# One hand-written order for six batches: every relu, square, sum and copy at a place of its own, and a PSUM bank named for each matmul group

## The chip, the cores and the metric

The kernel runs on one core of one Trainium2 chip. The metric is device time in microseconds (us), the median of the runs shown. Engines are called PE (TensorE, matmuls), DVE (VectorE), ACT (ScalarE), POOL (GpSimd) and SP (SyncE, here a queue that issues DMAs).

## The reference

There are 8 batches, 12 heads, 448 positions and a head size of 64; then a feed-forward layer over 3584 tokens, from 768 to 2048 and back to 768.

```python
scores = scale * np.matmul(q, k.transpose(0, 1, 3, 2))
attn = np.maximum(scores, 0.0) ** 2 / S
attn_out = np.matmul(attn, v)              # (B, H, S, D)
x = attn_out.transpose(0, 2, 1, 3).reshape(B * S, H * D)
h = x @ w_in
g = np.maximum(h, 0.0) + alpha * np.minimum(h, 0.0)
out = g @ w_out
```

## The kernel before

All work is written out in one order by hand. Each engine runs its own instructions strictly in the order in which they stand, and waits by semaphore for what other engines must give. So the order of the words in the plan strings is the order in every queue.

**Attention.** Four heads of one batch are a quad; there are 24 quads, three to a batch. `turn_dma` copies a quad's q and k into the tile `perm` (one buffer) and lets a DMA on SP's queue turn it into the tile `T`; `land` is a tiny POOL copy that waits for that DMA, and behind it POOL issues the loads of quads to come. A quad has seven chunks. A chunk (`c` in the plans, lines 204 to 221) is four matmuls of 64x64 weights that run side by side, here called one group of four, into two neighbouring PSUM banks (a pair); then a relu out of both banks, on ACT or DVE as the letter says; and, later, `s` squares it (line 229 or 231). When all seven chunks of a quad are squared, `v` (line 241) multiplies them with v: seven groups of four into one pair, and two copies (lines 253 and 255) take the pair to the tile `xT`, one bank on ACT and one on DVE.

**First layer.** When a batch's three quads are in `xT`, sixteen units `f` follow: six matmuls (line 275) into one bank, then ACT makes `neg` (line 281; two buffers) and DVE writes `gT` (line 282). `gT` holds two batches.

**Second layer.** The 28 tiles of 128 tokens are mostly taken in pairs. A pair is multiplied by a scheme with seven products of half size in place of eight: `p1` to `p7` on PE (line 335, 8 matmuls of 384 columns each), sums of parts of `gT` on DVE (`pa` to `pd`, line 331), and after each product a copy on ACT (lines 351 and 356) or an addition on DVE (line 340). Products 2, 3, 4 and 5 give blocks of the output, which `store` sends with two DMAs each. Four tiles go the plain way (`g`, line 300).

**PSUM.** There are 8 banks. `take_pair` gives the pair that was taken longest ago, `one` a single bank by the same rule. In the last six batches `one` first tries the other half of the pair that was used last (the flag `paired`), so that pairs stay whole. A plan word does a whole step at once: `cA` issues the matmuls and the relu, `f` the matmuls, `neg` and `gT`, `p6` the product and its addition.

**The order.** The first two batches and the start have plans of their own. Then batch by batch the strings `FIRST_PAIR`, `EACH`, `EACH`, `ONE_PAIR`, `EACH` and `LAST` run, each from `B`: its units `f` first, then its products, with the chunks of later quads in between, mostly three at a time (`cAAA`), and the three `v` of the next batch. This is `EACH`:

```python
EACH = """B f s0D f s0A f n f f f f s2A f s1D cAAA s1D f f s0D f s0A f p1 nD f f r1 f f s1A pc p2 pa r2 ra pb cA vDA s1D s0D cAA p6 s0D pd p7 n cA rc s1A cAA s0D s0A p5 p4 rb p3 cAAD v cAD s1D s1A s3A cA s3A r6 s2A r7 rd r5 s0A cAD r4 s0D r3 cAD v cD cA"""
LAST = """B f s0A f f f f s3A s2A s2A f f s2A f f f f f f pc f f s0A f p1 r1 pa pb p2 p6 p7 pd ra p5 rb rc p4 p3 r6 z r7 rd r5 r2 r3 r4e"""
```

Here `r` is the second pair of the batch, `n` is `turn_dma`, `land` and the next loads, `z` puts every second store from then on into ACT's queue, and `r4e` makes the last product in two parts, 256 and 128 columns wide. A `c` behind the last chunk, an `s` with nothing to square and an `n` behind the last quad do nothing.

Of the kernel before, what the change touches and what calls it, by code (L numbers as in the profile page):

```python
# [20 lines left out]
def kernel(  # L21
# [72 lines left out]

    def one():
        order = sorted(range(8), key=lambda i: (taken[i], i))
        free = [i for i in order if taken[i] < 10**9]
        if not paired:
            return order[0]
        mate = max(free, key=lambda i: taken[i]) ^ 1  # L100
        return mate if mate in order[:4] and taken[mate] < 10**9 else order[0]
# [86 lines left out]
    def turn_dma(n, eng="A"):  # L188
        if n in (5, 7, 8):
            w = w_mix[2 + n % 2].rearrange("p k c -> p (k c)")[:, :4 * NJ * D]  # L190
            p = w.rearrange("p (a j s d) -> p a j s d", a=2, j=NJ, s=2)
        else:
            p = perm_pool.tile([128, 2, NJ, 2, D], BF16, tag="perm", name="perm")
        for i, name in enumerate("qk"):
            (nc.vector.tensor_copy if eng == "D" else nc.scalar.copy)(p[:, i], raw.pop((n, name)).rearrange("p s j d -> p j s d"))  # L195
# [1 line left out]
        nc.sync.dma_start_transpose(out=t.rearrange("p a j c -> p (a j) c"),
                                    in_=p.rearrange("p a j s d -> p (a j s d)"))
# [35 lines left out]
    def attnv(n, eng="AD"):  # L234
        ps = take_pair()
        vv = vraw.pop(n)
        for j in range(NJ):
# [10 lines left out]
        if eng == "A":
            nc.scalar.activation(xT[b][:, g], ps[:, :, :S], ACTF.Copy, scale=out_scale)
            return  # L250
        for r in range(2):
            if eng[r] == "A":
                nc.scalar.activation(xT[b][:, g, r], ps[:, r, :S], ACTF.Copy, scale=out_scale)  # L253
            else:
                nc.vector.tensor_scalar(xT[b][:, g, r], ps[:, r, :S], out_scale, None, ALU.mult)  # L255
# [15 lines left out]
    gT = singles.tile([128, KF, 2 * S], BF16, name="gT")  # L271

    def f1_mm(ps, b, ff, ks):
        for km in ks:
            nc.tensor.matmul(ps, w_in_sb[:, km // 2, km % 2, bass.ts(ff, 128)],  # L275
                             xT[b][:, km // 2, km % 2, :],
                             start=(km == 0), stop=(km == KM - 1))

    def f1_out(ps, b, ff):
        neg = neg_pool.tile([128, S], F32, tag="neg", name="neg")  # L280
        nc.scalar.activation(neg, ps, ACTF.Relu, scale=-1.0)  # L281
# [11 lines left out]
    def f2(sb, c, h, parts=None):  # L293

        first_col, width = COLS[h][0], COLS[h][1] - COLS[h][0]
        o = o_pool.tile([128, d_model - CUT], F32, tag="o", name="osb")
        for lo, hi in parts or ((0, width),):
            ps = take_bank()[:, :hi - lo]
            for ff in range(KF):
                nc.tensor.matmul(ps, gT[:, ff, bass.ts(c, 128)], w_out_sb[:, ff, first_col + lo:first_col + hi],  # L300
                                 start=(ff == 0), stop=(ff == KF - 1))
            nc.scalar.copy(o[:, lo:hi], ps)
            store(sb, c, first_col + lo, first_col + hi, o[:, lo:hi])
# [11 lines left out]
    class Pair:  # L315

        def __init__(self, a, b):
            self.a, self.b = a, b
# [14 lines left out]
        def mm(self, ps, left, right, start):  # L333
            for i in range(KH):
                nc.tensor.matmul(ps, left[:, i], right[:, i], start=(start and i == 0), stop=(i == KH - 1),  # L335
                                 skip_group_check=not start)

        def plus(self, ps, u, keep=None):
            t = keep if keep is not None else o_pool.tile([128, d_model - CUT], F32, tag="o", name="osb")[:, :u.shape[-1]]
            nc.vector.tensor_tensor(t, ps, u, ALU.add)  # L340
            return t

        def kept(self, tag="u"):
            return u_pool.tile([128, NH], F32, tag=tag, name=tag)

        def p1(self):
            self.xb = hold()
            self.x = psum[:, self.xb, :NH]
            self.mm(self.x, self.a11, w_out_sb[:, :KH, :NH], True)
            self.m1 = self.kept("m")  # L350
            nc.scalar.copy(self.m1, self.x)

        def p2(self):
            self.mm(self.x, self.a12, w_out_sb[:, KH:, :NH], False)
            t = o_pool.tile([128, d_model - CUT], F32, tag="o", name="osb")[:, :NH]
            nc.scalar.copy(t, self.x)  # L356
            take(self.xb, 1)
            store(*self.a, 0, NH, t)

        def p6(self):  # L360
            y = take_bank()[:, :NH]
            self.mm(y, self.s[2], w_mix[1], True)
            self.u2 = self.plus(y, self.m1, self.kept())

        def p7(self):
            y = take_bank()[:, :NH]
            self.mm(y, self.s[3], w_mix[2], True)
            self.u3 = self.plus(y, self.u2, self.kept())

        def p5(self):  # L370
            self.zb = hold()
            self.z = psum[:, self.zb, :NH]
            self.mm(self.z, self.s[1], w_mix[0], True)
            store(*self.b, NH, d_model, self.plus(self.z, self.u3))

        def p4(self, parts=((0, NH),)):
            for lo, hi in parts:
                y = take_bank()[:, :hi - lo]
                self.mm(y, self.a22, w_mix[3][:, :, lo:hi], True)
                t = self.plus(y, self.u3[:, lo:hi])  # L380
                store(*self.b, lo, hi, t)

        def p4x(self, lo=0, hi=256):
            if lo == 0:
                self.o4 = o_pool.tile([128, d_model - CUT], F32, tag="o", name="osb")[:, :NH]
            y = take_bank()[:, :hi - lo]
            self.mm(y, self.a22, w_mix[3][:, :, lo:hi], True)
            self.plus(y, self.u3[:, lo:hi], self.o4[:, lo:hi])
            if hi == NH:
                store(*self.b, 0, NH, self.o4)  # L390

        def p4y(self):
            self.p4x(256, NH)

        def p4e(self):
            self.p4(((0, 256), (256, NH)))

        def p3(self):
            self.mm(self.z, self.s[4], w_out_sb[:, KH:, NH:], False)
            store(*self.a, NH, d_model, self.plus(self.z, self.u2))  # L400
            take(self.zb, 1)
# [150 lines left out]
```

## Time and profile before

| what | us |
|---|---|
| median of 3 runs | 373.29 (373.25 to 375.82) |
| span of the profiled execution | 371.3 |
| median of the runs less that span | 2.0 |
| start of batch 2's first `f` in the profile | 109.2 |

The profile is of one execution and its span runs from the first to the last instruction on the core. A matmul's time in it is longer than its distance to the next one, since matmuls are pipelined; what counts for PE is the distance from start to start. In a timeline a row begins with the start and the length of a run of like instructions; x48 says how many; brackets hold how long the engine was idle before and what released it.

### The profile page before, as it was taken

What the parts mean: (1) busy time and instruction counts of PE and PEld (TensorE: products, weight loads), DVE (VectorE), ACT (ScalarE), POOL (GpSimd) and SP (SyncE); (2) the same over time, 40 slices, a digit from 0 to 9 for tenths busy, and PEclk for the clock granted to TensorE, in tenths of its full rate; (3) what the DMA queues carried; (4) which work ended last, traced back from release to release, by engine and by line L of the source; (5) the groups of instructions that cost most, each with busy time, mean ns of one, the idle gap of its engine ahead of it and who ended that gap; (6) DMA issues with size and microseconds to landing.
All of it is one profiled execution on the core that took longest, in us unless ns stands there. A gap on an engine that the chain in (4) does not pass through costs nothing.

```text
span 371.3 us, 7894 instructions
## 1 busy us (share of the span) xinstructions
PE 363.6 (98%) x3105; PEld 197.5 (53%) x3105; DVE 278.0 (75%) x445; ACT 274.7 (74%) x406; POOL 71.7 (19%) x120
## 2 busy tenths in 40 slices
PE   8799999999999999999999999999999999999995
PEld 6454564444554565545555455554555455555563
DVE  3989988885968989566887768888749667856653
ACT  5998676877997678885997859967699866964400
POOL 8566150304211222022020220202200000000000
PEclk9999999999999999999999999999999999999999
DMA  9999989999999868455882659727646201220024
GB/s 143 188 203 202 199 135 191 153 160 167 180 171 150 123 96 163 92 89 90 160 144 64 99 80 168 144 56 121 111 89 134 49 2 43 65 65 0 0 64 108
DMA packets 73557, 43.29 MB, mean 117 GB/s; under 512 B 40368, under 2 KB 73008, under 8 KB 73520
## 3 DMA queue, kind: packets, MB, share of 16 engines
q0 software_dynamic: 27136, 22.58, 42.0%
q1 hardware_dynamic: 45712, 19.61, 25.9%
q10 hardware_dynamic: 672, 0.59, 0.5%
q8 instruction: 24, 0.39, 0.4%
q14 instruction: 13, 0.11, 0.1%
HBM read 45.62 MB, written 11.01 MB: 153 GB/s over the span
## 4 chain that ended last, share of the span: by engine, by line
PE 94%; DVE 2%; ACT 2%; issue 1%; ACTq 0%
PE psum L275 38%; PE psum L335 30%; PE psum L241 9%; PE psum L209 9%; PE psum L300 6%; PE psum L183 1%; PE psum L165 1%; DVE gT L282 1%; ACT rl L218 1%; ACT xT L253 1%; ACT neg L281 1%; DVE w_mix L195 1%; DVE T L186 0%; DVE at L231 0%; DVE osb L340 0%
## 5 line engine op out<-in xcount | busy, mean ns | idle before, releaser
L275 PE MATMUL psum<-xT,w_in_sb 128*128 128x448 bf16 x768 | 150.4, 353 | 0.2 <-DVE gT L282 0.2
L282 DVE SCALAR_TENSOR_TENSOR gT<-neg,beta_sb,psum 128x448 bf16<-128x448 f32 x128 | 85.3, 679 | 43.4 <-ACT neg L281 42.1
L218 ACT ACTIVATE rl<-psum 128x896 bf16<-128x896 f32 x128 | 111.2, 925 | 6.7 <-PE psum L209 4.7
L275 PEld LDWEIGHTS <-w_in_sb 128*128 128x128 bf16 x768 | 73.4, 98 | 73.0 <-issue 6.8
L281 ACT ACTIVATE neg<-psum 128x448 f32<-128x448 f32 x128 | 68.5, 547 | 41.0 <-PE psum L275 32.7
L231 DVE TENSOR_TENSOR at<-rl 128x896 bf16<-128x896 bf16 x105 | 62.2, 620 | 0.5 <-ACT rl L218 0.2
L229 ACT ACTIVATE at<-rl 128x896 bf16<-128x896 bf16 x63 | 58.6, 952 | 0.3
L335 PEld LDWEIGHTS <-S 128*128 128x128 bf16 x384 | 36.7, 98 | 28.4 <-issue 5.3
L335 PE MATMUL psum<-w_mix,S 128*128 128x384 bf16 x288 | 49.8, 326 | 0.2
L220 DVE TENSOR_SCALAR rl<-psum 128x896 bf16<-128x896 f32 x40 | 43.2, 1086 | 8.7 <-PE psum L209 8.1
L209 PE MATMUL psum<-T 64*64 64x448 bf16 x672 | 45.9, 357 | 2.0 <-DVE T L186 1.0
L418 POOL COPY landed<-T 1x1 bf16<-1x1 bf16 x18 | 3.3, 181 | 206.1 <-DMA T<-perm 182.9
L335 PEld LDWEIGHTS <-gT 128*128 128x128 bf16 x296 | 28.3, 98 | 20.2 <-issue 1.8
L241 PE MATMUL psum<-at,vraw 64*64 64x448 bf16 x672 | 36.6, 350 | 0.0
L335 PE MATMUL psum<-w_out_sb,gT 128*128 128x384 bf16 x192 | 34.0, 326 | 0.0
L340 DVE TENSOR_TENSOR osb<-psum,u 128x384 f32<-128x384 f32 (+2 forms) x37 | 20.2, 547 | 12.6 <-PE psum L335 8.2
L209 PEld LDWEIGHTS <-T 64*64 64x64 bf16 x672 | 17.4, 105 | 22.7 <-issue 14.8
L241 PEld LDWEIGHTS <-vraw 64*64 64x64 bf16 x672 | 21.2, 106 | 11.9 <-issue 2.9
L300 PE MATMUL psum<-w_out_sb,gT 128*128 128x256 bf16 (+1 forms) x128 | 22.0, 326 | 0.1
L255 DVE TENSOR_SCALAR xT<-psum 128x448 bf16<-128x448 f32 x24 | 14.9, 622 | 8.9 <-PE psum L241 8.3
L253 ACT ACTIVATE xT<-psum 128x448 bf16<-128x448 f32 x24 | 13.3, 556 | 9.1 <-PE psum L241 8.7
L356 ACT COPY osb<-psum 128x384 f32<-128x384 f32 x12 | 5.8, 480 | 17.4 <-PE psum L335 17.4
(45 smaller groups left out, 242.0 us busy)
## 6 DMA issues: line engine op xcount, KB each, us to landing
out_dram<-osb SPq DMA_DIRECT2D x91, 96.0 KB, 2.2
vraw<-in_v_dram POOLq DMA_DIRECT2D x24, 224.0 KB, 6.5
qraw<-in_q_dram POOLq DMA_DIRECT2D x23, 224.0 KB, 4.1
kraw<-in_k_dram POOLq DMA_DIRECT2D x23, 224.0 KB, 5.3
w_in_sb<-in_moe_w_in_dram POOLq DMA_DIRECT2D x16, 192.0 KB, 8.0
w_out_sb<-in_moe_w_out_dram POOLq DMA_DIRECT2D x4, 512.0 KB, 9.5
w_out_sb<-in_moe_w_out_dram POOLq DMA_DIRECT2D x4, 256.0 KB, 8.8
out_dram<-osb SPq DMA_DIRECT2D x8, 128.0 KB, 3.2
```

The lines of the kernel that those rows point to most:

```text
L209: nc.tensor.matmul(ps[64 * c:64 * c + 64, r, :S], t[64 * r:64 * r + 64, 1, j, 64 * c:64 * c + 64], t[64 * r:64 * r + 64, 0, :, 64 * c:64 * ...
L218: nc.scalar.activation(rl, ps[:, :, :S], ACTF.Relu)
L220: nc.vector.tensor_scalar(rl, ps[:, :, :S], 0.0, None, ALU.max)
L229: nc.scalar.activation(a, rl, ACTF.Square)
L231: nc.vector.tensor_tensor(a, rl, rl, ALU.mult)
L241: nc.tensor.matmul(ps[64 * s:64 * s + 64, r, :S], vv[64 * r:64 * r + 64, s, j, :], a[64 * r:64 * r + 64, s], start=(j == 0), stop=(j == NJ ...
L275: nc.tensor.matmul(ps, w_in_sb[:, km // 2, km % 2, bass.ts(ff, 128)], xT[b][:, km // 2, km % 2, :], start=(km == 0), stop=(km == KM - 1))
L281: nc.scalar.activation(neg, ps, ACTF.Relu, scale=-1.0)
L282: nc.vector.scalar_tensor_tensor(gT[:, ff, (b % 2) * S:(b % 2) * S + S], neg, beta_sb[:, ff:ff + 1], ps, ALU.mult, ALU.add)
L300: nc.tensor.matmul(ps, gT[:, ff, bass.ts(c, 128)], w_out_sb[:, ff, first_col + lo:first_col + hi], start=(ff == 0), stop=(ff == KF - 1))
L335: nc.tensor.matmul(ps, left[:, i], right[:, i], start=(start and i == 0), stop=(i == KH - 1), skip_group_check=not start)
L340: nc.vector.tensor_tensor(t, ps, u, ALU.add)
```

## The change

The plans of the start and of batches 0 and 1 stay as they are, word for word in effect. The six strings from `FIRST_PAIR` to `LAST` are replaced by one list, `P[4]`, for which a class `Line` has one short function per operation. Each operation has a word of its own, and a digit names the bank:

```diff
+        def do_f(self, w):          # "f4": six matmuls into bank 4
+            i = int(w)
+            self.bank[i] = self.b, self.ff, psum[:, i, :S]
+            f1_mm(psum[:, i, :S], self.b, self.ff, range(KM))
...
+        def do_N(self, w):          # "N4": neg of bank 4, on ACT
...
+        def do_G(self, w):          # "G4": gT from bank 4, on DVE
...
+        def do_c(self, w):          # "c6": chunk into banks 6 and 7
+        def do_r(self, w):          # "r6A": its relu, on ACT
+        def do_s(self, w):          # "sD": the oldest open square, on DVE
+        def do_v(self, w):          # "v2": into banks 2 and 3
+        def do_x(self, w):          # "x20A": bank 2's half to xT, on ACT
+        def do_k(self, w):          # "kqD", "kkD": copy of q or of k into perm
+        def do_t(self, w):          # transpose DMA, land, the next loads
...
+        def product(self, w):       # "+b63": pair b, product 6, bank 3
+        def output(self, w):        # "-b6": its copy or addition, and its store
+        def mix(self, w):           # "*bc": one sum of parts of gT
+        def do_g(self, w):          # "g2505": plain tile, bank 5;  "h5": its copy
```

The pairs of tiles are the same twelve, called a to l. The list:

```
*bc f0 sA *ba N0 *bb f1 f2 +b63 kqA f4 kkD G0 N1 sA N2 G1 sA c6 N4 G2 -b6 c0 c2 r6A sD G4 f5 r0A f4 N5 N4 sD f6 sD G5 f7 t c0 G4 sA N6 r2D N7 G6 kqD
c4 r0A r4A sD v2 kkA c0 x20A f6 sD x21A f4 N6 sD f5 G7 f7 r0D G6 N4 t c2 N5 G4 G5 sD N7 r2A G7 c0 c4 r0A sD f6 f7 f2 f3 sD N6 N7 G6 kqD r4A N2 sD G7
kkA c0 c4 r0A v6 N3 G2 r4D x60A G3 *bd c0 x61D r0A sA sD t c4 +b72 +b53 -b7 c0 c6 sA sD r4A r0A sA +c12 r6D -b5 sA +b44 +b33 c6 r6A *ca sD kqD -b4 c0
-c1A v4 kkD x40A r0D c6 t -b3 r6D c0 x41A +c22 sD -c2A sA sD f3 r0D c4 N3 f2 r4A c6 sD G3 c0 r6D c4 r0A kqD kkD sA *cc f3 f0 f1 N3 N2 G3 t N1 G2 N0
r4A sD G1 f6 N6 f7 f1 G0 f0 sD N7 G6 G7 c2 c4 N1 G1 v6 r2A c2 r4D kqD N0 c4 r2A x60A f1 r4A f2 N1 sD f3 sD kkD sD G0 x61A G1 N2 c4 c6 sD f0 sD f1 r4A
N3 G2 r6A f2 G3 f3 N0 *cb c4 N1 G0 G1 sD sA N2 r4A N3 c6 G2 v0 r6D x00A G3 c4 t c6 x01A r4A +c72 +c63 *da r6A kqD sD +c50 sD sA -c6 -c7 *cd sA -c5 c4
kkD r4A c6 *db *ea sD t c2 r6A +d11 +c44 c6 -c4 r2A +c30 sD sA c2 r6A -d1A sD r2D c4 r4A -c3 v6 x60A *dc c4 c2 x61D +d60 sD +d21 r4D -d6 c6 r2A c2 *dd
kqD c4 sA +d70 r6A kkD +d56 -d2A +d47 -d7 sA sA r2D sA -d5 r4A sD +d36 c0 sA r0D -d3 c2 v4 sD r2A x40A c0 -d4 c2 sA f6 r0A f7 r2D x41A N6 *eb sD c2 sD
c0 N7 t r2A f4 G6 N4 f5 sA G4 r0D N5 G5 G7 sD f6 f2 f3 N6 c0 N2 v4 G6 r0A N3 c6 c0 G2 r6A r0A f2 f6 kqD f7 sA x40D kkD sD x41A *ec f0 G3 N6 G6 N7 N2
f1 G7 N0 G2 c4 G0 N1 G1 c6 c2 f0 r4A f1 N0 G0 +e14 r6A f5 r2D N1 sA c6 G1 -e1A sD c2 c0 N5 r6D sA t G5 sD +e24 f6 +e67 r2A sD r0A N6 c2 kqA r2A c0
-e2D v4 sA sD G6 r0D kkA c2 -e6 sD r2D c0 *ed r0A x40A +e76 sD +e47 t *fa -e7 *fb c2 +e50 +f11 -e5 sA x41A -f1D +e30 -e4 c4 sA c6 r2A sA *fc v2 r4D
kqD c4 r6A x20A r4A c6 kkD +f21 sD sD x21A +f64 c2 r6A c6 -f2A sD -e3 sD *fd c0 r2A +f75 +f52 +f43 r6D t sD r0A sA c0 sD -f6 -f7 c6 v4 -f5 r0A x40A c0
r6D x41A *ga sA c6 r0D -f4 +f32 r6A f4 N4 f5 sA c0 sD r0A c6 -f3 N5 kqD G4 *gb r6A c2 f4 sD f0 f1 r2D G5 N4 kkA sD f5 G4 f4 N0 N1 G0 G1 sD sA N5 N4 c2
c6 v0 r2A G5 r6D sD c2 c6 f5 r2A x00D G4 f2 x01A N5 f3 c0 r6A G5 N2 c4 sD N3 c6 G2 r0A sD G3 t f2 r4A f3 sD N2 r6D c0 *gc G2 sD sA N3 sD c4 f6 r0A f7
G3 f2 N6 f3 c0 kqD r4A N7 G6 c4 G7 N2 v6 N3 G2 r0D r4A c4 kkA G3 sD r4A x60A sD c0 sA +g12 -g1D t +g63 r0A -g6 +g74 x61A c0 *gd sD sA g2505 +g22 sD c6
r0A h5 c0 -g7 sD r6A v4 c6 r0D c0 *ha *hb r6D x40D x41D sA g2513 +g56 h3 c4 r0D -g2D c0 c2 *hc +g47 r4D r0D f4 +h15 sA r2D N4 f0 -g5 N0 +h61 sD -h1D
+h72 -g4 +h53 f7 +g36 *hd -h6 -g3 f1 -h7 +h25 -h5 +h46 -h4 f2 +h33 f6 G4 N1 G0 G1 f4 -h3 f0 f1 N7 f3 G7 N6 f7 G6 N1 N3 -h2D f6 G1 N4 sD G3 N0 f5 G0 sD
sA N7 G4 sA G7 f3 N6 v0 +i14 f7 x00D x01D -i1A N3 f0 G6 G3 N7 f1 G7 N0 N2 +i24 G0 f3 N5 f0 G5 f5 N0 G2 *ic *ia -i2D *ib +i72 *ja f4 +i66 N4 -i6 -i7
+j17 +i56 +i42 *id -i5 -i4 *jb +i36 G4 f2 G0 f4 -i3 f0 N2 f6 N1 G1 N4 f1 G4 -j1D *jc G2 N0 +j64 N3 f2 G3 N6 G6 N5 f3 G0 N1 G1 +j76 f0 G5 f1 f5 N1 G1
-j6 N5 G5 +j27 *jd +j41 f4 N0 N3 +l15 G3 N2 -j2A G0 +j53 N4 G2 G4 -j7 -l1A *ka -j5 +k10 *lc +j33 +l72 *kc *kb +k74 *la +k67 *lb -j4 -k1A -j3 +k46 *kd
-k6 -k7 +k51 +l63 -k5 +k31 *ld -k4 -l6 +l54 -k3 +k20 -l7 -l5 -k2D +l47 -l4 +l34 +l25 z -l3 -l2A
```

Copies out of products 1 and 2 can now be on DVE (`-e1A` and `-g1D`). The last pair's product 4 is one group again. `z` now stands ahead of the last two outputs. Everything else is bookkeeping: `hold_pair`, the flag `paired` and the old methods of `Pair` go, `attnv` and `f2` are cut into a part for the matmuls and a part for what follows, and assertions watch that nothing is read too early while the program is built.

More of the change, by code (lines that the diff above doesn't have):

```diff
@@ L97, in one @@
         free = [i for i in order if taken[i] < 10**9]
[L98 to L101, printed above, removed]
+        return free[0]
     def take_bank():
@@ L271, with batches_of, may_write, may_read @@
     gT = singles.tile([128, KF, 2 * S], BF16, name="gT")
+    f1_done = {}
+    f2_done, f2_half = set(), set()
+    readers = {b: 0 for b in range(B)}
+    def batches_of(sb, c):
+        return {2 * sb + (128 * c) // S, 2 * sb + (128 * c + 127) // S}
+    for tile_no in range(B // 2 * NJ):
+        for b in batches_of(*divmod(tile_no, NJ)):
+            readers[b] += 1
+    def may_write(b, ff):
+        assert b < 2 or readers[b - 2] == 0, "gT is still read"
+        f1_done[(b, ff)] = True
+    def may_read(t, halves=(0, 1)):
+        for b in batches_of(*t):
+            for h in halves:
+                assert all((b, ff) in f1_done for ff in range(KF // 2 * h, KF // 2 * h + KF // 2)), "gT is not written"
+    def has_read(*tiles):
+        for t in tiles:
+            for b in batches_of(*t):
+                readers[b] -= 1
     def f1_mm(ps, b, ff, ks):
         for km in ks:
+            assert x_done[b] >= km // 2 + 1
+            f1_mm_done[b] = f1_mm_done.get(b, 0) + 1
             nc.tensor.matmul(ps, w_in_sb[:, km // 2, km % 2, bass.ts(ff, 128)],
@@ L291, in store, with f2_mm, f2_out, f2 @@
             eng.dma_start(out=rows[j][:, lo:hi], in_=t[64 * u:64 * u + 64])
-    def f2(sb, c, h, parts=None):
-        first_col, width = COLS[h][0], COLS[h][1] - COLS[h][0]
-        o = o_pool.tile([128, d_model - CUT], F32, tag="o", name="osb")
[L297 to L303, printed above, removed]
+    def f2_mm(sb, c, h, i):
+        may_read((sb, c))
+        if (sb, c) in f2_half:
+            f2_done.add((sb, c))
+            has_read((sb, c))
+        f2_half.add((sb, c))
+        lo, hi = COLS[h]
+        for ff in range(KF):
+            nc.tensor.matmul(psum[:, i, :hi - lo], gT[:, ff, bass.ts(c, 128)], w_out_sb[:, ff, lo:hi],
+                             start=(ff == 0), stop=(ff == KF - 1))
+    def f2_out(sb, c, h, i):
+        lo, hi = COLS[h]
+        o = o_pool.tile([128, d_model - CUT], F32, tag="o", name="osb")
+        nc.scalar.copy(o[:, :hi - lo], psum[:, i, :hi - lo])
+        store(sb, c, lo, hi, o[:, :hi - lo])
+    def f2(sb, c, h):
+        i = one()
+        take(i, 1)
+        f2_mm(sb, c, h, i)
+        f2_out(sb, c, h, i)
+    mixed = [0] * 4
     def weight_mix(i, lo, hi):
+        assert not i or mixed[{1: 0, 2: 0, 3: 1}[i]] > mixed[i]
+        mixed[i] += 1
         b11, b12 = w_out_sb[:, lo:hi, :NH], w_out_sb[:, lo:hi, NH:]
@@ L318, in __init__ @@
             self.a, self.b = a, b
+            self.done, self.made, self.ps, self.t, self.held = 0, [], {}, {}, {}
             ga, gb = gT[:, :, bass.ts(a[1], 128)], gT[:, :, bass.ts(b[1], 128)]
@@ L321, in __init__, with product @@
             self.s = {}
+        def product(self, name, ps):
+            need = {"1": "", "2": "1", "6": "b", "7": "c", "5": "a", "4": "", "3": "5d"}[name]
+            assert all(x in self.made for x in need) and name not in self.made
+            assert name not in "5674" or mixed[{"5": 0, "6": 1, "7": 2, "4": 3}[name]] == 2
+            if name in "124":
+                may_read(self.b if name == "4" else self.a, (name != "1",))
+            left, right, start = {"1": (self.a11, w_out_sb[:, :KH, :NH], True),
+                                  "2": (self.a12, w_out_sb[:, KH:, :NH], False),
+                                  "6": (self.s.get(2), w_mix[1], True), "7": (self.s.get(3), w_mix[2], True),
+                                  "5": (self.s.get(1), w_mix[0], True), "4": (self.a22, w_mix[3], True),
+                                  "3": (self.s.get(4), w_out_sb[:, KH:, NH:], False)}[name]
+            for i in range(KH):
+                nc.tensor.matmul(ps, left[:, i], right[:, i], start=(start and i == 0), stop=(i == KH - 1),
+                                 skip_group_check=not start)
+            self.ps[name] = ps
+            self.made.append(name)
+            self.done += 1
+            if self.done == 7:
+                has_read(self.a, self.b)
@@ L323, in mix @@
         def mix(self, *which):
             for i in which:
+                for t, halves in {1: ((self.b, (0, 1)),), 2: ((self.a, (0,)),), 3: ((self.a, (0,)), (self.b, (0,))),
+                                  4: ((self.a, (1,)),)}[i]:
+                    may_read(t, halves)
+                assert i != 4 or "6" in self.made
+                self.made.append("abcd"[i - 1])
                 t = self.s[2] if i == 4 else S_pool.tile([128, KH, 128], BF16, tag="S", name="S")
@@ L331, in mix @@
                 nc.vector.tensor_tensor(t, x, y, op)
[L333 to L401, printed above, removed]
+        def run(self, name):
+            if name in "23":
+                i = self.held.pop({"2": "1", "3": "5"}[name])
+                take(i, 1)
+            elif name in "15":
+                i = self.held[name] = hold()
+            else:
+                i = one()
+                take(i, 1)
+            self.product(name, psum[:, i, :NH])
+            self.output(name)
@@ L422, in __init__ @@
         def __init__(self):
-            self.b, self.ff, self.held, self.parts, self.p, self.r, self.quad = 0, 0, [], 0, None, None, 11
+            self.pairs = [Pair(*t) for t in (((0, 3), (0, 4)), ((0, 5), (0, 6)), ((1, 0), (1, 1)), ((1, 2), (1, 3)),
+                                             ((1, 4), (1, 5)), ((1, 6), (2, 0)), ((2, 1), (2, 2)), ((2, 3), (2, 4)),
+                                             ((2, 6), (3, 0)), ((3, 1), (3, 2)), ((3, 3), (3, 4)), ((3, 5), (3, 6)))]
+            self.b, self.ff, self.held, self.parts, self.quad = 0, 0, [], 0, 11
         def __call__(self, plan):
@@ L517, with __init__, __call__, do_h @@
-    ONE_PAIR = """B f f nD s2A s0A s2D f s1D f f f s1D f f s0A f f cAD s1D cA s0D n s0D f f f f f f pc pa g50 pb cADA v p1 cAAA s0A p6 s2D s0A p2 pd p7 s1A p5 n s0A p4 p3 s0D cADA s0D v cAD s1A s2A cD s2A s1D g51 s0D cDAD v cD cA cA"""
-    LAST = """B f s0A f f f f s3A s2A s2A f f s2A f f f f f f pc f f s0A f p1 r1 pa pb p2 p6 p7 pd ra p5 rb rc p4 p3 r6 z r7 rd r5 r2 r3 r4e"""
-    for b, plan in ((2, FIRST_PAIR), (3, EACH), (4, EACH), (5, ONE_PAIR), (6, EACH), (7, LAST)):
-        walk.p, walk.r = ([walk.r] if b == 2 else []) + [Pair(*t) for t in pairs[b][b == 2:]] + [None] * (b == 5)
-        walk(plan)
+    class Line:
+        def __init__(self, walk):
+            self.pairs, self.bank, self.b, self.ff, self.quad = walk.pairs, {}, walk.b, walk.ff, walk.quad
+            self.perm = None
+        def __call__(self, plan):
+            for word in plan.split():
+                getattr(self, {"+": "product", "-": "output", "*": "mix"}.get(word[0], "do_" + word[0]))(word[1:])
+        def do_f(self, w):
+            if self.ff == KF:
+                self.b, self.ff = self.b + 1, 0
+            i = int(w)
+            self.bank[i] = self.b, self.ff, psum[:, i, :S]
+            f1_mm(psum[:, i, :S], self.b, self.ff, range(KM))
+            self.ff += 1
+        def do_N(self, w):
+            b, ff, ps = self.bank[int(w)]
+            neg = neg_pool.tile([128, S], F32, tag="neg", name="neg")
+            nc.scalar.activation(neg, ps, ACTF.Relu, scale=-1.0)
+            self.bank[int(w)] = b, ff, ps, neg
+        def do_G(self, w):
+            b, ff, ps, neg = self.bank.pop(int(w))
+            may_write(b, ff)
+            nc.vector.scalar_tensor_tensor(gT[:, ff, (b % 2) * S:(b % 2) * S + S],
+                                           neg, beta_sb[:, ff:ff + 1], ps, ALU.mult, ALU.add)
+        def do_c(self, w):
+            i = int(w)
+            n, j = stream.pop(0)
+            self.bank[i] = n, j
+            score_mm(n, j, psum[:, i:i + 2])
+        def do_r(self, w):
+            i = int(w[0])
+            n, j = self.bank.pop(i)
+            late.append((n, j, relu(psum[:, i:i + 2], w[1])))
+        def do_s(self, w):
+            square(*late.pop(0), w)
+        def do_v(self, w):
+            i, n = int(w), turn["v"]
+            turn["v"] += 1
+            attnv_mm(n, psum[:, i:i + 2])
+            self.bank[i] = [n, 0]
+        def do_x(self, w):
+            i, r, eng = int(w[0]), int(w[1]), w[2]
+            attnv_out(self.bank[i][0], psum[:, i:i + 2], r, eng)
+            self.bank[i][1] += 1
+            if self.bank[i][1] == 2:
+                del self.bank[i]
+        def do_k(self, w):
+            if self.perm is None:
+                self.perm = perm_pool.tile([128, 2, NJ, 2, D], BF16, tag="perm", name="perm")
+            copy = nc.vector.tensor_copy if w[1] == "D" else nc.scalar.copy
+            copy(self.perm[:, "qk".index(w[0])], raw.pop((self.quad, w[0])).rearrange("p s j d -> p j s d"))
+        def do_t(self, w):
+            n = self.quad
+            assert (n, "q") not in raw and (n, "k") not in raw
+            turn_rows(n, self.perm)
+            self.perm = None
+            land(n)
+            if n + 2 < NQ:
+                load_qk(n + 2)
+            if n + 1 < NQ:
+                load_v(n + 1)
+            self.quad += 1
+        def product(self, w):
+            self.pairs["abcdefghijklmn".index(w[0])].product(w[1:-1], psum[:, int(w[-1]), :NH])
+        def output(self, w):
+            self.pairs["abcdefghijklmn".index(w[0])].output(w[1], w[2:])
+        def mix(self, w):
+            self.pairs["abcdefghijklmn".index(w[0])].mix("abcd".index(w[1]) + 1)
+        def do_g(self, w):
+            sb, c, h, i = map(int, w)
+            f2_mm(sb, c, h, i)
+            self.bank[i] = sb, c, h
+        def do_h(self, w):
+            f2_out(*self.bank.pop(int(w)), int(w))
+        def do_z(self, w):
+            two_queues.append(1)
@@ new lines @@
+sA N7 G4 sA G7 f3 N6 v0 +i14 f7 x00D x01D -i1A N3 f0 G6 G3 N7 f1 G7 N0 N2 +i24 G0 f3 N5 f0 G5 f5 N0 G2 *ic *ia -i2D *ib +i72 *ja f4 +i66 N4 -i6 -i7
++j17 +i56 +i42 *id -i5 -i4 *jb +i36 G4 f2 G0 f4 -i3 f0 N2 f6 N1 G1 N4 f1 G4 -j1D *jc G2 N0 +j64 N3 f2 G3 N6 G6 N5 f3 G0 N1 G1 +j76 f0 G5 f1 f5 N1 G1
+-j6 N5 G5 +j27 *jd +j41 f4 N0 N3 +l15 G3 N2 -j2A G0 +j53 N4 G2 G4 -j7 -l1A *ka -j5 +k10 *lc +j33 +l72 *kc *kb +k74 *la +k67 *lb -j4 -k1A -j3 +k46 *kd
+-k6 -k7 +k51 +l63 -k5 +k31 *ld -k4 -l6 +l54 -k3 +k20 -l7 -l5 -k2D +l47 -l4 +l34 +l25 z -l3 -l2A"""
+    for i in range(4):
+        walk(P[i])
+    Line(walk)(P[4])
+    assert all(p.done == 7 for p in walk.pairs)
+    assert not stream and not late and turn["v"] == NQ and f2_done == {(0, 0), (0, 1), (0, 2), (2, 5)}
```

93 lines of the change are left out of this document (50 added, 43 removed).

## The prediction

> **What bounds the kernel now.** I read the page first, for the busiest engine and for the chain of work that ended last.
>
> ```profile
> span 371.3 us, 7894 instructions
> PE 363.6 (98%) x3105; PEld 197.5 (53%) x3105; DVE 278.0 (75%) x445; ACT 274.7 (74%) x406; POOL 71.7 (19%) x120
> ...
> PE 94%; DVE 2%; ACT 2%; issue 1%; ACTq 0%
> ```
>
> PE is busy 98% of the span and makes 94% of the chain. A busy PE need not be a PE at its peak, so the next view is the busy time by stretch, and then a timeline of one long batch, for the distances between matmuls.
>
> ```profile
> core 0: us, PE busy (x) PEld busy (x) DVE busy (x) ACT busy (x) POOL busy (x), PEclk, DMA share, GB/s
> ...
> 109.20:152.40 43.20, 43.14 (x364) 23.32 (x360) 36.24 (x59) 33.14 (x49) 10.04 (x17) 1.00 0.85 139
> ...
> 349.20:371.30 22.10, 18.37 (x121) 11.39 (x119) 10.93 (x20) 2.46 (x5) 0.00 (x0) 1.00 0.28 72
> 109.20:349.20 240.00, 239.76 (x1917) 128.46 (x1914) 178.21 (x281) 185.25 (x273) 29.74 (x52) 1.00 0.53 94
> ```
>
> The clock is granted in full. DVE and ACT are busy 74% and 77% of the 240 us. The stretch that the change orders anew begins at 109.2.
>
> ```profile
> 198.45 9.26 PE L275 MATMUL psum<-xT,w_in_sb 128*128 128x448 bf16 x48
> ...
> 207.63 0.76 PE L209 MATMUL psum<-T 64*64 64x448 bf16 x12
> ...
> 208.33 4.71 PE L275 MATMUL psum<-xT,w_in_sb 128*128 128x448 bf16 x24
> ...
> 212.88 1.46 PE L335 MATMUL psum<-w_out_sb,gT 128*128 128x384 bf16 x8
> ...
> 232.13 0.76 PE L209 MATMUL psum<-T 64*64 64x448 bf16 x12
> ...
> 232.85 1.52 PE L241 MATMUL psum<-at,vraw 64*64 64x448 bf16 x28
> ...
> 234.17 0.77 PE L209 MATMUL psum<-T 64*64 64x448 bf16 x12
> ...
> 234.40 0.54 ACT L253 ACTIVATE xT<-psum 128x448 bf16<-128x448 f32 x1
> ...
> 234.99 4.06 PE L335 MATMUL psum<-w_mix,S 128*128 128x384 bf16 x24
> ```
>
> These rows give all prices on PE. A matmul of `f` follows the last after (212.88 - 208.33) / 24 = 0.190 us. A product's matmul lasts 0.326 us and 24 span 4.06: (4.06 - 0.33) / 23 = 0.162 each. Seven groups of four of `v` take 234.17 - 232.85 = 1.32: 0.189 a group, and I take a chunk's group for the same. From 198.45 to 208.33 PE made 48 matmuls and three groups: 9.88 - 48 x 0.190 - 3 x 0.189 leaves 0.2 us. That is the price of a **round trip** from full-width matmuls to groups of four of 64x64 and back.
>
> Two more losses stand in these rows. From 232.13, three groups take 0.57, yet `v` starts 0.72 later; from 234.17, three groups and a round trip's half take 0.67, yet the product starts 0.82 later, just after ACT's copy at line 253 (234.40 and 0.54) has emptied the bank. So 0.15 us each is **a wait for a bank** that was given out too soon: the least recently used rule hands it on after only three groups.
>
> **The old stretch, as a sum.** By the plan strings PE makes 576 matmuls of `f` (109.4), 75 products of 8 (97.2), 99 + 15 x 7 = 204 groups (38.6) and two plain tiles.
>
> ```profile
> 109.25 9.19 PE psum L275 x48
> ...
> 263.53 1.75 PE psum L300 x16
> ...
> 280.05 3.56 PE psum L300 x16
> ...
> 367.61 0.29 DVE osb L340
> ```
>
> This is the chain in order of time; the plain tiles are 5.3, so plain matmul work is 250.5. I count 28 runs of `c` and `v` words between words of full width: 28 x 0.2 = 5.6, or 5.9 at 0.21. By following the rule through the strings I find 14 places where a bank comes back with only 0.57 to 0.66 us of matmul work between: 14 x 0.15 = 2.1. Sum 258.5; measured, from 109.2 to the addition at 367.6 that ends the chain, 258.4. So **nearly all is plain matmul work**, which the change keeps in full. It can win at most the 2.1, and it can add trips and waits.
>
> **The change, part by part.**
>
> *Round trips.* The new list has 34 runs of `c` and `v` against 28, since chunks come one or two at a time: 6 x 0.21 = **+1.3**. Below, the 6 could cost nothing where PE waits anyway. The Trainium skill, "TensorEngine Tiling (Array Packing)", Key Properties, says that a change of tiling mode drains TensorE; this bears on the 0.2. With the constant of "TensorE: Matmul & The Clock Gate", Single matmul latency, 398 cycles at 2.4 GHz, an estimate would be 0.17 for each drain, 0.33 a trip and 2.0 in all; the trace's 0.2 decides.
>
> *Banks.* In the new list no bank comes back with less than 1.3 us of matmul work between. A wait like that at 234.99 needs under some 0.8. So the 14 short returns go: **-2.1**; at worst as many come back elsewhere: 0.
>
> *The start.* The first word on PE is `f0`. Bank 0 is half of the pair of the `v` just before.
>
> ```profile
> 108.90 0.54 ACT L253 ACTIVATE xT<-psum 128x448 bf16<-128x448 f32 x1
> 109.02 0.62 DVE L255 TENSOR_SCALAR xT<-psum 128x448 bf16<-128x448 f32 x1 [1.19 <-PE psum L241]
> ...
> 109.18 9.25 PE L275 MATMUL psum<-xT,w_in_sb 128*128 128x448 bf16 x48
> ```
>
> The old first `f` used another bank and began at 109.18; the new one waits for ACT until 109.44: **+0.3**. Bank 1 is free at 109.64, before `f1`.
>
> *Work moved from ACT to DVE.* Counting letters, DVE gets 9 relus, 12 squares, 11 copies of q or k and 9 copies of products, and loses 7 copies to `xT`.
>
> ```profile
> L282 DVE SCALAR_TENSOR_TENSOR gT<-neg,beta_sb,psum 128x448 bf16<-128x448 f32 x128 | 85.3, 679 | 43.4 <-ACT neg L281 42.1
> L231 DVE TENSOR_TENSOR at<-rl 128x896 bf16<-128x896 bf16 x105 | 62.2, 620 | 0.5 <-ACT rl L218 0.2
> L220 DVE TENSOR_SCALAR rl<-psum 128x896 bf16<-128x896 f32 x40 | 43.2, 1086 | 8.7 <-PE psum L209 8.1
> ...
> L331 DVE TENSOR_TENSOR S<-gT 128x1024 bf16<-128x1024 bf16 x24 | 15.9, 685 | 0.0
> ...
> L255 DVE TENSOR_SCALAR xT<-psum 128x448 bf16<-128x448 f32 x24 | 14.9, 622 | 8.9 <-PE psum L241 8.3
> ...
> L195 DVE COPY perm<-qraw 128x896 bf16<-128x896 bf16 x5 | 3.1, 612 | 0.0
> ...
> L340 DVE TENSOR_TENSOR u<-psum,m 128x384 f32<-128x384 f32 x12 | 6.7, 557 | 6.3 <-PE psum L335 3.4 <-ACT rl L218 2.6
> ```
>
> That is 9 x 1.09 + 12 x 0.62 + 11 x 0.61 + 9 x 0.56 - 7 x 0.62 = +25 us on DVE, on top of 178.2 + 10.9: 214 of 258, 83%. It is not spread evenly: the new list ends its chunks after 170 us of matmul work, the old after 210. Up to the word `+g47`, 172 us into it, DVE has 33 relus, 63 squares, 64 `gT`, 19 copies, 6 to `xT`, 31 outputs and 27 sums: 169 us by the durations above, on 172 of PE. But durations overlap:
>
> ```profile
> 209.05 1.16 DVE L231 TENSOR_TENSOR at<-rl 128x896 bf16<-128x896 bf16 x2
> ...
> 211.31 1.27 DVE L282 SCALAR_TENSOR_TENSOR gT<-neg,beta_sb,psum 128x448 bf16<-128x448 f32 x2 [1.10 <-ACT neg L281]
> ```
>
> Two squares in 1.16, two `gT` in 1.27: each but the first takes 0.09 less. 243 operations x 0.09 = 22, so 147 us of 172, 86%: as much as the 84% (36.24 of 43.2) that the old list carries in its first 43 us with PE at full rate. I cost it at nothing, with PE's own work as the cover.
>
> How thin that cover gets, I worked out where `f0` and `f1` come twice in a row (`f7 ... f0 ... f1 ... f0`, 97 us into the list). Counted from the end of `f7`: first `f0` ends 1.14, `f1` 2.28, three chunks and half a trip 2.95: then `f0` wants bank 0 again. ACT makes `N7` and `N2` by 1.1 and `N0` when `f0` is out of the pipeline, 1.3 to 1.85; DVE makes `G7` from 0.8, `G2`, and `G0` from 2.0 to 2.7. Cover 0.2 us. It holds, but there are 62 of 280 groups where the words queued between on one engine are longer than the matmul work between. I take 2 such misses of 0.2: **+0.4**; bounds 0 and, for 62 x 0.09, 5.6.
>
> *Transposes and loads.* SP and POOL keep their instructions but for two stores of the last product; 13 transposes move within the order.
>
> ```profile
> L197 SPq DMA_TRANSPOSE T<-perm x13: 1296/1525/3163, 114.0 to 292.5; - x13
> ...
> DMA to landing us min/median/max: 3.9/4.0/7.0
> ```
>
> Shortest from the copy of k to the first chunk that needs `T`: quad 23, some 7 us (`kkA` at 155, `c6` at 162.6); the stores that stand before that `t` on SP have their data long before. Loads are issued two transposes ahead, 12 us or more. Nothing. If 7.0 came there, it would just be used up.
>
> *The end.* Old: the last product is made in two parts.
>
> ```profile
> 366.09 1.48 PE L335 MATMUL psum<-w_mix,gT 128*128 128x256 bf16 x16
> ...
> 366.93 1.80 SPq L291 DMA_DIRECT2D out_dram<-osb  x3
> 367.16 0.74 DVE L340 TENSOR_TENSOR osb<-psum,u 128x256 f32<-128x256 f32 x2 [0.26 <-PE psum L335]
> ```
>
> ```profile
> L356 ACT COPY osb<-psum 128x384 f32<-128x384 f32 x12 | 5.8, 480 | 17.4 <-PE psum L335 17.4
> ```
>
> New: eight of 384, 0.1 longer through the pipeline, and ACT's copy (0.48) for an addition of 0.29: +0.3. But SP then has two stores behind it in place of three, and the old third one began no earlier than about 368.1, where the new one does. 0.
>
> **Sum.** +1.3 - 2.1 + 0.3 + 0.4 = -0.1 on a span of 371.3: 371.2; with the 2.0 between span and median, **373.2 us**. A measurement of this kernel tells about 1% (3.7 us) from no change.
>
> **Rivals.**
>
> 1. *All cover holds* and the added trips fall where PE would wait: -2.1 + 0.3 and at best no trips: 371.5, or 371.1 without the start's wait. For it: the 14 short returns are certain to go. Against it: a PE that seldom waits hides no trips. 15%; within 1%.
>
> 2. *DVE becomes the bound* (slower). From the point at which an operation that arrives late pushes the next, each waits for its input, as the 42.1 us behind `neg` already do, and the 0.09 of overlap are lost where it counts: 169 us on 172 leave no room, and 62 tight groups pay 0.09 each, 5.6, in place of 0.4: 378.4. For it: the 0.2 of cover above. Against it: 84% on DVE for 43 us without harm. 20%.
>
> 3. *DVE takes no overlap at all.* The Trainium skill, "VectorE: DVE Perf Modes", The DRAIN you can't avoid, says the next operation does not start until the pipe is empty; it also says that one which isn't held starts earlier. As a mechanism here: every operation at its duration, 44.6 us on the first 43 of PE, and later stretches with no slack to win it back: 1.6 more than rival 2, 380. The rows of two above speak against it. 2%.
>
> 4. *Transposes land late*: two quads 1.5 us late, 376. 5%; within 1%.
>
> My forecast has 55%, with a range of its own from 372 to 375. 3% stays for something unseen that makes it faster.
>
> **Range and chances.** The range takes in rivals 1, 2 and 4: 371.1 to 378.4. Faster by over 1% would need a gain of 3.7 where all waits together are 2.1: 3%. Slower by over 1%: rivals 2 and 3, 22%, and 1% for a worse landing: 23%. Within 1%: 74%.
>
> **What would show it.** PE's matmul row counts are unchanged and its chain shows no piece of ACT line 253 between chunk and product (banks right). DVE's busy time rises to 80% or more, ACT's falls to some 66%. The first `f` begins about 109.5. If rival 2 is right, the waits list PE behind DVE's `gT` or relu for over 4 us. The prediction is wrong if the waits behind `T` or behind stores grow past 2 us, or if a round trip costs PE more than 0.2 where chunks stand singly.

## The result, and the profile after

The changed kernel takes 378.90 us in the median (375.60 to 385.11, 6 runs), the kernel before 373.27: the ratio is 1.0128, 95% interval 1.0095 to 1.0162; the run of 385.11 us, over 2% above the kernel's fastest, counts as slow and is left out of this ratio, as such runs are of every ratio below. In a second set of runs it was 377.05 against 373.02, ratio 1.0126 (1.0089 to 1.0164). So it is **slower by some 1.3%**, 4 to 5 us; the forecast was 373.2, with a range up to 378.4, which the median of the first set passes and that of the second does not. The profiled execution is the fastest of the six, with a run of 375.60 us.

The page of the kernel after, busy time and the chain that ended last:

```profile
span 373.7 us, 7817 instructions
PE 363.0 (97%) x3094; PEld 194.5 (52%) x3097; DVE 295.4 (79%) x478; ACT 245.4 (66%) x372; POOL 72.2 (19%) x120
...
PE 87%; DMA 4%; DVE 4%; ACT 2%; issue 1%; ACTq 0%; DVEq 0%; SPq 0%; POOLq 0%
PE psum L303 34%; PE psum L379 29%; PE psum L206 9%; PE psum L237 8%; PE psum L330 6%; DMA T<-perm 3%; DMA kraw<-in_k_dram 1%; DVE gT L311 1%; ACT rl L215 1%; DVE at L228 1%; DVE perm L584 1%; ACT neg L310 1%; DVE w_mix L188 1%; PE psum L175 1%; DVE rl L217 0%
```

PE's share of the chain went from 94% to 87%, and a name is new in it: DMA `T<-perm`, the transpose of a quad. Busy time by stretch says where:

```profile
109.20:152.40 43.20, 43.03 (x358) 21.85 (x358) 40.35 (x64) 35.80 (x55) 12.55 (x21) 1.00 0.88 138
152.40:195.40 43.00, 41.27 (x382) 21.62 (x380) 36.34 (x61) 33.59 (x50) 7.05 (x13) 1.00 0.81 119
195.40:238.40 43.00, 43.00 (x365) 22.28 (x364) 37.49 (x60) 35.17 (x53) 6.98 (x12) 1.00 0.64 110
```

The first number behind the comma is PE's busy time: it lacks 1.7 us between 152 and 195 and nothing in the stretch after. The chain in order of time (start, length, what) shows the place:

```profile
147.19 1.24 PE psum L303 x6
148.43 0.34 PE psum L206 x4
148.79 0.93 DVE rl L217
149.72 0.08 issue
149.80 1.15 DVE perm L584 x2
...
151.09 10.48 DMA T<-perm
...
161.69 0.62 DVE perm L584
162.31 1.07 DVE at L228 x2
163.38 0.53 DVE perm L584
163.90 0.53 DVE at L228
164.44 0.60 DVE gT L550
165.04 0.04 issue
165.08 4.70 PE psum L303 x24
```

DVE copies quad 15 into `perm` at 149.80; the transpose starts at 151.09 and lands only after 10.48 us; the copy of quad 16's q into the same, single buffer stands in DVE's queue and cannot start before 161.69. Behind it stand two squares, the copy of k, a third square and a `gT`, and for that `gT` PE waits. The waits, and PE's row with what released it, give the sizes:

```profile
DVE perm L584 <- DMA T<-perm: 2.9, 1, 2.9
...
165.08 1.11 PE L303 MATMUL psum<-xT,w_in_sb 128*128 128x448 bf16 x5 [1.69 <-DVE gT L550]
```

DVE lost 2.9 us, PE 1.7. And the transposes themselves, from 109 to 175 us, first before, then after (least, median, most):

```profile
DMA to landing us min/median/max: 4.0/4.3/7.0
...
DMA to landing us min/median/max: 5.3/6.6/10.5
```

### The profile page after: what moved, and what is told of

It reads as the page before. It is cut to its first block, busy times and chain, and to the rows that moved or that the text cites. A ratio compares the mean times of both kernels' runs of the same rounds, so it can differ in the third digit from the quotient of the medians.

```text
span 373.7 us, 7817 instructions
## 1 busy us (share of the span) xinstructions
PE 363.0 (97%) x3094; PEld 194.5 (52%) x3097; DVE 295.4 (79%) x478; ACT 245.4 (66%) x372; POOL 72.2 (19%) x120
## 4 chain that ended last, share of the span: by engine, by line
PE 87%; DMA 4%; DVE 4%; ACT 2%; issue 1%; ACTq 0%; DVEq 0%; SPq 0%; POOLq 0%
PE psum L303 34%; PE psum L379 29%; PE psum L206 9%; PE psum L237 8%; PE psum L330 6%; DMA T<-perm 3%; DMA kraw<-in_k_dram 1%; DVE gT L311 1%; ACT rl L215 1%; DVE at L228 1%; DVE perm L584 1%; ACT neg L310 1%; DVE w_mix L188 1%; PE psum L175 1%; DVE rl L217 0%
## 5 line engine op out<-in xcount | busy, mean ns | idle before, releaser
L303 PE MATMUL psum<-xT,w_in_sb 128*128 128x448 bf16 x768 | 153.1, 353 | 2.1 <-DVE gT L550 1.7
L215 ACT ACTIVATE rl<-psum 128x896 bf16<-128x896 f32 x119 | 105.2, 930 | 15.6 <-PE psum L206 15.3
L550 DVE SCALAR_TENSOR_TENSOR gT<-neg,beta_sb,psum 128x448 bf16<-128x448 f32 x96 | 63.3, 676 | 17.9 <-ACT neg L544 17.2
L228 DVE TENSOR_TENSOR at<-rl 128x896 bf16<-128x896 bf16 x117 | 69.1, 618 | 0.6 <-ACT rl L215 0.4
L217 DVE TENSOR_SCALAR rl<-psum 128x896 bf16<-128x896 f32 x49 | 53.0, 1086 | 13.3 <-PE psum L206 12.9
L206 PE MATMUL psum<-T 64*64 64x448 bf16 x672 | 47.0, 357 | 1.7 <-ACT rl L215 1.0
L226 ACT ACTIVATE at<-rl 128x896 bf16<-128x896 bf16 x51 | 48.1, 958 | 0.2
L396 DVE TENSOR_TENSOR osb<-psum,u 128x384 f32<-128x384 f32 x36 | 19.8, 552 | 11.9 <-PE psum L379 10.7
L237 PEld LDWEIGHTS <-vraw 64*64 64x64 bf16 x672 | 20.0, 107 | 12.5 <-issue 1.7
L311 DVE SCALAR_TENSOR_TENSOR gT<-neg,beta_sb,psum 128x448 bf16<-128x448 f32 x32 | 21.0, 678 | 3.9 <-ACT neg L310 3.3
L249 ACT ACTIVATE xT<-psum 128x448 bf16<-128x448 f32 x31 | 16.9, 558 | 5.0 <-PE psum L237 4.6
```

The costliest lines, as they stand in the source:

```text
L206: nc.tensor.matmul(ps[64 * c:64 * c + 64, r, :S], t[64 * r:64 * r + 64, 1, j, 64 * c:64 * c + 64], t[64 * r:64 * r + 64, 0, :, 64 * c:64 * ...
L215: nc.scalar.activation(rl, ps[:, :, :S], ACTF.Relu)
L217: nc.vector.tensor_scalar(rl, ps[:, :, :S], 0.0, None, ALU.max)
L226: nc.scalar.activation(a, rl, ACTF.Square)
L228: nc.vector.tensor_tensor(a, rl, rl, ALU.mult)
L237: nc.tensor.matmul(ps[64 * s:64 * s + 64, r, :S], vv[64 * r:64 * r + 64, s, j, :], a[64 * r:64 * r + 64, s], start=(j == 0), stop=(j == NJ ...
```

## The experiments

Theory 1: the new list prepares its quads closer together while loads are still thick; a transpose lands late, the single buffer `perm` stays taken, and the next copy holds up a whole in-order engine. Rival: DVE has too much to do, or the order itself (trips, thin cover) costs the time.

**after_again**: no edit.

> The changed kernel once more, for a second profile and for the spread of its times. Theory 1 (one buffer perm: the next quad's copy of q, in line on DVE, waits until the DMA has turned the last quad's perm, which is late where loads run at the same time): 375 to 380 us, with a DVE or ACT wait at the copy into perm behind DMA T<-perm of 2 to 7 us in total, other transposes than in the first profile perhaps. Rival (DVE has too much to do): the same time, but PE's lost time is spread over many places behind gT and relu, and the waits behind DMA T<-perm stay under 3 us.

Measured: 377.05 us, ratio as above. The waits of its profile:

```profile
DVE perm L584 <- DMA T<-perm: 4.6, 3, 2.2
```

Three waits now, with transposes that land after 7.3 to 8.9 us in that stretch. The place and the size move from run to run, the kind does not; PE's two idle times behind a `gT` in it, 1.04 us before 156.00 and 0.99 before 165.63, follow the two longest of these waits.

**sq_act**:

```diff
-... sD ... (every fifth, 12 in all, before 171 us of matmul work)
+... sA ...
```

> Every fifth square of DVE in the first 171 us of matmul work goes to ACT: 12 squares, 6.4 us off DVE at 0.53 each. Theory 1: the copies into perm still wait for the DMA, 376 to 380, no change beyond 1 us. Rival (DVE has too much to do): the time falls by 3 us or more, to 373 to 375.

Measured: 379.79 us, ratio 1.0148 (1.0093 to 1.0202). 6.4 us off DVE brought nothing; this interval and that of the changed kernel overlap for most of their width. The squares put some 11.5 us on ACT (12 x 0.96), so this run alone does not clear DVE's load; the next one does. The waits were still there: in its profile, that of the run of 385.02 us, five copies stand behind DMA `T<-perm`, 16.1 us in all.

**perm2**:

```diff
-tc.tile_pool(name="perm", bufs=1)   # v: bufs=6, o: bufs=6
+tc.tile_pool(name="perm", bufs=2)   # v: bufs=5, o: bufs=5
```

> perm gets a second buffer; to make room the tiles of v go from 6 to 5 buffers and those of the output from 6 to 5. Theory 1: the waits of the copies behind DMA T<-perm are gone, 372 to 375, if the fifth output buffer is not missed (a DVE wait behind DMA out_dram<-osb would show that). Rival (DVE has too much to do): 377 to 380.

Measured: 373.77 us (10 runs), ratio 1.0015 (0.9982 to 1.0047): no difference from the kernel before, 3.3 us better than the changed kernel on the same chip in the same set. DVE has the same work in both, so **DVE's load is not the cause**. Its profiled execution was its slowest, 378.06, and shows what is next in line:

```profile
DVE perm L584 <- DMA qraw<-in_q_dram: 3.4, 1, 3.4
```

Its chain leads to that copy:

```profile
132.85 9.57 DMA T<-perm
...
143.76 10.35 DMA kraw<-in_k_dram
```

No copy waits for `perm` any more, but here quad 13's transpose, from 132.85, landed after 9.6 us, so POOL's `land` and the loads of quad 15 behind it came late. These took 10 us themselves, and quad 15's copies waited for q and k instead; PE stood idle for 3.1 us before 157.71.

**v5o5**: the same without the second `perm`.

```diff
-tc.tile_pool(name="v", bufs=6)      # o: bufs=6
+tc.tile_pool(name="v", bufs=5)      # o: bufs=5
```

> The changed kernel with 5 buffers for v and 5 for the output in place of 6 each, and one for perm: what the kernel with two perm buffers had beside them. Theory 1: as the changed kernel, 376 to 380, so that the gain was perm's. Rival: fewer buffers hold back the loads and so make room for the transposes: 373 to 375.

Measured: 379.15 us, ratio 1.0146 (1.0103 to 1.0189). So the gain of the kernel above was `perm`'s. Its waits:

```profile
DVE perm L584 <- DMA T<-perm: 5.2, 2, 4.2
```

**fewer_loads**:

```diff
-            if n + 1 < NQ:
+            if 12 <= n + 1 <= 17:
+                vraw[n + 1] = vraw[11] if n == 11 else self.kept
+                self.kept = vraw[n + 1]
+            elif n + 1 < NQ:
                 load_v(n + 1)
```

> The changed kernel without the loads of v for quads 12 to 17, which read quad 11's v instead: a third of the loads between 110 and 175 us is left out, perm has one buffer as before. If the transposes land late because loads run at the same time: they land in under 7 us each in that stretch, the waits behind DMA T<-perm fall under 1 us and the time to 372.5 to 374.5. If the one buffer is too little whatever the loads do: waits and time stay as they were, 376 to 380.

This kernel leaves out the loads of v for quads 12 to 17 and multiplies with quad 11's v in their place, so only its time and its waits mean anything. Measured: 374.33 us, ratio 1.0035 (1.0017 to 1.0053), with one buffer. Its transposes from 109 to 175 us:

```profile
DMA to landing us min/median/max: 4.0/5.2/7.1
```

In its profile (span 371.5) no copy into `perm` waits for a DMA. So the transposes land late **because of the loads beside them**: a third of the loads away, the stores as they were, and the longest landing is 7.1 in place of 10.5. The longest alone would say little, since it runs from 7.6 to 13.4 in the profiles of the new list with all its loads. But quads 12 and 13 land after 4.0 us each here, after 5.3 and 5.6 in the changed kernel, and after 5.1 or more in every other profile of the new list with all its loads. And the landing of 10.5 us belongs to a transpose that started at 151.09, within 0.8 us of the three loads that POOL issued at 150.31, 151.02 and 151.73. Either remedy, a second buffer or fewer loads, takes back most of the loss.

**spaced**:

```diff
-... kqD kkD sA *cc f3 f0 f1 N3 N2 G3 t ...     (quad 15; so for 16, 17, 18)
+... sA *cc f3 f0 f1 N3 N2 G3 kqD kkD t ...
```

> The copies and the transpose of quads 15 to 18 stand later in the list (at 43, 58, 71 and 82 us of matmul work in place of 39, 49 to 60, 63 and 75), nothing else changes. Theory 1: no engine waits behind DMA T<-perm for over 0.3 us but POOL's land; the time falls by 3 to 6 us, to 373 to 375, and the spread goes. Rival (DVE has too much to do): DVE's work is the same, 377 to 380.

Measured: 376.62 us, ratio 1.0127 (1.0068 to 1.0186): a miss. In its profile the waits of quads 15 to 18 are gone, as expected; quad 11's copy, which was not moved, waited 1.4 us. But PE has new losses where the moved copies now stand, before 171.63, 186.83 and 197.75. The waits list them in one line:

```profile
PE psum L206 <- DVE rl L217: 1.1, 3, 0.5
```

Two copies of 0.53 us each, put ahead of a relu, delay a chunk by 0.3 to 0.5. Counted from start to start of its matmuls, PE loses 1.7 us around these three places and 0.8 at 116.5, behind quad 11's copy. The rival has a grain of truth: **the list has no room for a foreign microsecond** on DVE.

**before_tight**, the other way round: the old list, with one word moved.

```diff
-r1 f pc s0A f f f f f f p6 r2 cADA s1D v cAA ra s0D pd cA p7 rb n p5
+r1 f pc s0A f f f f n f f p6 r2 cADA s1D v cAA ra s0D pd cA p7 rb p5
```

> The kernel before, with one word moved: the copies, the transpose and the loads of quad 13 come after the fourth of six units in place of behind the sum rb, some 7 us of matmul work after those of quad 12 in place of 16. Theory 1: ACT waits 2 to 4 us at the copy into perm behind DMA T<-perm or behind the load, the units behind it wait too, and the time rises by 1.5 to 4 us, to 374.5 to 377. Rival (the new list is slow because of its order on DVE and its round trips, not because of the spacing of transposes): 373, no change.

Measured: 376.76 us in the median, ratio 1.0064 (1.0038 to 1.0090), some 2.4 us by the ratio. Its chain:

```profile
123.98 5.74 DMA T<-perm
...
129.78 0.07 ACT perm L195
...
130.63 0.93 ACT perm L195
131.56 0.45 ACT neg L281
...
132.04 1.28 DVE gT L282 x2
...
133.37 0.34 PE psum L335
```

The same chain, made in the kernel before: transpose, copy (on ACT here, 1.5 us late), `neg`, `gT`, PE, which stands idle for 0.8 us in this profile, that of its best run (374.58). Quad 13's transpose, moved up among the loads, lands after 10.5 us, where it took 4.0 in the kernel before. So moving one quad's copies, transpose and loads closer to the last quad's does it, with everything else in the old order.

**perm2_merged**:

```diff
-f3 r0D c4 N3 f2 r4A c6
+f3 r0D f2 c4 N3 r4A c6
-c6 -c4 r2A +c30 sD sA c2
++c30 c6 -c4 r2A sD sA c2
-c2 +e50 +f11 -e5 sA x41A -f1D +e30 -e4 c4
+   +e50 +f11 -e5 sA x41A -f1D +e30 -e4 c2 c4
-c0 *gd sD sA g2505 +g22 sD c6
+   *gd sD sA g2505 +g22 sD c0 c6
```

> The new list with two perm buffers (and 5 for v and for the output), and four single chunks moved next to another chunk (one unit, one product and two chunks change places), so that there are 30 round trips in place of 34. At 0.2 us a trip the time falls by 0.8 from the 373.8 of the kernel with two perm buffers, to 373.0; if a trip costs nothing because PE would wait there, it stays at 373.8; if the moved chunks come too late for their squares, it rises.

Measured: 376.95 us, ratio 1.0103 (1.0084 to 1.0122): slower than with the chunks apart. Four trips fewer should have won 0.8; instead each move made PE wait for a relu on ACT, 0.70, 0.64, 0.64 and 0.83 us, and no copy waits for `perm` here. PE and ACT at the first of the four:

```profile
147.63 0.76 PE L206 MATMUL psum<-T 64*64 64x448 bf16 x12
...
148.13 1.73 ACT L215 ACTIVATE rl<-psum 128x896 bf16<-128x896 f32 x2 [0.90 <-PE psum L206]
...
149.10 0.38 PE L206 MATMUL psum<-T 64*64 64x448 bf16 x4 [0.70 <-ACT rl L215]
```

The next chunk needs the pair that a relu of 0.92 us is still emptying. A chunk that stands alone in this list buys the time for the relu before it: 0.2 us for the trip against 0.6 to 0.8 for the wait.

No version here beats the kernel before; the nearest is the one with two `perm` buffers.

## Why the prediction was wrong

*What bounds the kernel.* Right. With the waits for `perm` out of the way, the time is that of before within the interval (373.77 against 373.02); the sum of the other terms, -0.1, had nearly said so. The two profiles differ by 2.4 us (373.7 and 371.3), and the terms as measured below add up to that: -1.4 for the banks, +1.2 for the trips (6 x 0.2), +0.3 for the start, +0.2 for a late relu, +0.4 for the end and +1.7 for the wait behind `perm`. Without the last they come to +0.7 where I had -0.1; the banks and the end make the difference.

*Round trips.* Right. A round of three groups between units and a product, from PE's timeline after:

```profile
215.12 1.30 PE L303 MATMUL psum<-xT,w_in_sb 128*128 128x448 bf16 x6
216.35 0.76 PE L206 MATMUL psum<-T 64*64 64x448 bf16 x12
217.05 1.48 PE L379 MATMUL psum<-w_out_sb,gT 128*128 128x384 bf16 x8
```

From 215.12 to 217.05 is 1.93; less 6 x 0.190 and 3 x 0.189 leaves 0.22. The trace has 34 such rounds from 109 us on, as counted, and 28 before.

*Banks.* Right in kind, but too large: no piece of a copy to `xT` stands in the chain between a chunk and a product from 110 us on; the 0.15 us waits are gone. By the distances from start to start, the trace before has ten of them from 109 us on, 1.4 us in all, where I had counted 14 and 2.1. That was the change's whole gain, and the trips take back most of it.

*The start.* Right: PE stands idle for 0.25 us before the first unit, behind ACT's copy, and starts it at 109.37 in place of 109.18.

*Work moved to DVE.* Right in the main: DVE is busy 295.4 us (79%) and ACT 245.4 (66%), against 278.0 and 274.7. That is 17 us more on DVE, where I had added 25 by durations, which overlap; over the first 172 us of the list DVE is busy 151.0, 88%, against the 86% that I had worked out. Costing it at nothing was right for the load, as the run with two `perm` buffers shows. Of the two misses of 0.2 us one can be seen: at 171.84 PE starts a chunk 0.2 us late, behind a relu on DVE. The cover that I worked out at 0.2 us holds where nothing disturbs the order, and nowhere more: see the runs with moved copies and moved chunks. The 0.09 us pushes of rival 2 were not what came.

*Transposes and loads.* **This is the step that failed.** I priced them at "Nothing", from the copy of k to the first chunk that needs `T`, and found cover enough, rightly: in the profile after no chunk waited for `T`. I did not price the other reader of the same event: the next quad's copy, which needs the one buffer `perm` back. The transposes of quads 14, 15 and 16 start at 143.17, 151.09 and 164.07, the last one put off by this very wait (it starts at 160.83 in the run with fewer loads). So the list leaves about 8 and 10 us from one to the next, and the copy of q comes before that. I allowed for a landing of 7.0 us, the longest of the 13 before, which only the first two, the ones in the thick of the loads, had taken; in the new list one took 10.5. The new list puts six transposes between 109 and 165 us where there were four, each with its loads behind it. My lead for the loads, 12 us or more, has the same gap: POOL issues them behind `land`, so a late landing shortens it, and this is what the profile with two buffers shows.

So rival 4, transposes that land late, was the right kind, but with the wrong waiter, at 3 us with 5%. One of my signs of being wrong came: waits behind `T` of more than 2 us, 2.9 in the first profile and 4.6 in the second. Measured, between the changed kernel and the one with two buffers: 3.3 us in the median. In the profiles PE stood idle behind it for 1.7 us in the first and 2.0 in the second, more where the clock falls too (below).

*The end.* A small miss: from the end of PE's last matmul to the end of the span it is 4.1 us, against 3.7 before, so +0.4 in place of 0.

## What to carry to other kernels

When a list is made denser, ask of every DMA not only when its result is needed but when its source buffer is needed back, which in-order engine will wait for that, and which loads are issued only after it lands. A median landing time over a whole stretch says little: take the landings from the part where the loads run, and expect them to grow when more transfers are moved there. And before merging or moving anything in a just-in-time order, find which relu or copy the gap was for.

## What the runs showed of the hardware that I had not expected

A transpose that lands in 4.0 us in a quiet stretch took 5 to 11 us beside loads. The Trainium skill, "DMA: Bandwidth & Descriptors", Queues, rings and completion order, says that each DMA engine takes turns between its queues packet by packet; that fits, since leaving out a third of the loads brought quads 12 and 13 from 5.3 and 5.6 us to 4.0; no run here shows the turns themselves.

A wait costs more than its length once it is long. In the run with 5 buffers for v and output and one for `perm` PE stood still for 3.0 us before 166.56; its timeline and the stretches before and after:

```profile
166.56 5.76 PE L303 MATMUL psum<-xT,w_in_sb 128*128 128x448 bf16 x15 [3.01 <-DVE gT L550]
```

```profile
160.00:166.50 6.50, 3.55 (x25) 1.61 (x23) 3.33 (x7) 2.44 (x5) 2.33 (x4) 0.92 0.63 69
166.50:171.50 5.00, 4.94 (x14) 2.05 (x14) 4.05 (x8) 3.30 (x6) 0.00 (x0) 0.50 1.19 184
172.50:177.50 5.00, 5.00 (x61) 2.63 (x60) 3.93 (x6) 3.56 (x7) 2.33 (x4) 1.00 0.55 71
```

The granted clock (the last column but two) falls to 0.50 and comes back by 172.5: 15 matmuls take 5.76 us where (15 - 1) x 0.19 + 0.35 = 3.0 would do, so 2.7 us on top of the 3.0. The Trainium skill, "TensorE: Matmul & The Clock Gate", Why this matters for your kernels, warns of idle gaps over some 3 us; the trace agrees at 3.0, and again at 3.1 in the profile with two `perm` buffers, where the clock was 0.50 from 157.7 to 160.7. The waits of 1.0 to 1.7 us in the two profiles of the changed kernel left the clock at 1.00. This may be part of why the changed kernel's times spread: in its second set the runs of 376.1 and 376.3 us had a mean clock of 0.999 or more, those of 377.8 and 379.2 one of 0.994. It is not all of it, for in the first set two runs of 378.4 us had 0.999 and 1.000.
